# Attention with normalised queries and keys, then a gated block: one raw load placed behind two turns, and 16 more idle products

## The chip, the core and the metric

The kernel runs on one core of a Trainium2 chip. The core has a matrix engine (TensorE, PE in the profile; its weight loads are shown as PEld), a vector engine (VectorE, DVE), a scalar engine (ScalarE, ACT), a general engine (GpSimd, POOL) and SyncE (SP), which here only issues DMAs. Each engine works through its own list in order and waits on semaphores for the others. DMAs move data between the main memory, SBUF and, for the turns below, within SBUF.

The metric is the device time of one execution in microseconds (us). Before the change, three timed runs gave 277.88, 278.66 and 277.12 us, with a median of 277.88.

## The reference

Inputs are q, k and v of 8 batches, 12 heads, 448 positions and 64 numbers, and the weights of a gated block with a model width of 768 and an inner width of 1024. What is computed, cut to its core:

```
q_n = q / sqrt(mean(q*q) + 1e-6) * g_q          # over the 64 numbers; k likewise
scores = q_n @ k_n^T / 8;  attn = softmax(scores);  x = attn @ v     # heads side by side: 768 wide
h = max(x @ w_in, 0);  u, v2 = first and second 512 columns of h
v_n = (v2 - mean) / sqrt(var + 1e-6)            # over the 512 columns
gated = u * (w_spatial @ v_n + b_spatial)
out = gated @ w_out
```

The output has 8 x 448 x 768 float32 numbers.

## The kernel before

The heads are worked in 24 groups of four: group G is batch G // 3, heads 4 (G % 3) and up. A group has two raw tiles of 128 partitions x 896 float32, i = 0 for q and i = 1 for k. Each is one DMA of 448 KB.

The order of the work is written out by hand in the string `PLAN`. The loop at the end of the kernel goes through its words; each word calls the function `op_` plus its first name, and appends instructions to the lists of the engines concerned. A word such as `L.10.0/7` has the operation, its numbers (group 10, tensor 0), then the buffer or the PSUM banks, then a letter for the engine if there is a choice (a ScalarE, v VectorE, g GpSimd). So the order of the words sets the order of the instructions within every engine, and that of the DMAs in SyncE's list. Between engines there are only semaphores.

What the words mean that matter here:

- `L.G.i/slot` (line 296): a raw load of q or k of group G into one of ten raw buffers, by SyncE. `l` (line 309) is the same by halves, for group 0.
- `Q` (lines 392 and 394): the square, on ScalarE, VectorE or GpSimd. `R` (line 405) sums it, `I` and `J` (lines 418 and 423) make one over the root by a logarithm and an exponential on ScalarE. `N` (line 438) multiplies raw data by it into one of four bf16 buffers, nrm.
- `P` and `K` (lines 457, 474 to 476): for groups 0 to 3, TensorE transposes nrm and an engine copies the result out to a query or key tile.
- `T.G.i/slot` (line 493): the turn, for groups from 4 on. A transposing DMA, issued by SyncE, goes from nrm to a query tile, qT, or to a turned key tile, kr. It takes the place of `P`.
- `Z.G` (line 476): multiplies the turned keys by the two gains into the key tile kT, on VectorE or ScalarE.
- `S` (line 518): scores on TensorE, with keys on the partitions. `E` (line 526): their exponentials on ScalarE, into one of 22 tiles, et. `s`, `a` and `b` (line 553): sums and products with v on TensorE. `D`, `d`, `X` (lines 572, 576, 582): the division, into xt.
- `V`, `W`, `U`, `H`, `O` (lines 598, 627, 664, 678, 692): the gated block's products on TensorE, with `c`, `u`, `B`, `A`, `G`, `o` between them on VectorE and ScalarE. `t` stores an output tile.
- `v` (line 326), `wi` (line 333), `wo` (line 340): loads of v and of weights, issued by GpSimd.
- `z.n/f` (line 261): n idle products on an identity tile, of 128 x 64, into a spare corner of a PSUM bank. Their result is not read. The first four words of this kind stand in the first line of the plan and make one burst of 11 + 24 + 7 + 5 = 47 products.

Square, normalisation and copy of different engines are also kept in the plan's order where they use a shared port: `port` adds a semaphore between consecutive ones of VectorE and GpSimd.

SyncE's list around the change is, in order: L.10.0, L.9.1, T.4.0, T.4.1, L.8.0, T.5.1, T.5.0, L.8.1, L.11.0, L.11.1, T.6.0, T.6.1. L.10.0 is the load of the queries of group 10 into raw buffer 7. T.4.0 turns the queries of group 4, the first group that is turned by DMA, and T.4.1 its keys. The reader of L.10.0 is `Q.10.0/0/g`, a square on GpSimd.

Of the kernel before, what the change touches and what calls it, by code (L numbers as in the profile page):

```python
# [19 lines left out]
SINGLES = 4  # L20

PLAN = """
setup//v l.1.0/0 l.0.0/1 q.0.0/0/a q.1.0/1/a r.0.0//v r.1.0//v i.0//a j.0//a n.0.0//v z.11/f z.24/f z.7/f z.5/f
gl.0//g l.0.1 n.1.0//v l.1.1 q.0.1//a gl.1//g gA//v q.1.1//v r.1.1//v gB/3 L.1.1/2 r.0.1//v i.1//a Q.1.1/2/v L.1.0/3
j.1//a z.13/f Q.1.0/1/a gC//v L.2.0/4 n.0.1//v z.20/f ws//g L.2.1/5 p.1.0/2 Q.2.0/0/a p.0.0/1 Y.2/0 R.1.1//v Y.3/6
Y.0/3 k.1.0/0/v z.9/f R.1.0//v y.2//v z.8/f R.2.0//v z.4/f k.0.0/0/a y.3//v S.0.1/45 y.0//v I.1//a z.3/f J.1//a
# [8 lines left out]
b.0.1.0/0 L.12.1/8 b.0.4.0 S.2.2/12 wi.0.0//g b.1.3.0 b.1.2.0 I.4//a a.1.4.0 E.2.2/e/a s.0.2.0/4 s.0.3.0 J.4//a d.1//a  # L35
R.5.1//v s.0.4.0 S.2.4/56 a.1.3.0 wi.1.0//g E.2.4/f/a b.0.2.0 N.4.0/2/v S.2.0/12 s.0.0.0 E.2.0/g/a X.1.0//v s.0.5.0
s.0.1.0 s.0.6.0 D.0/1/a b.0.6.0 P.3.0/6 K.3.0/3/v P.3.1/5 K.3.1/3/v wi.0.2//g b.0.0.0 S.2.1/12 S.2.5/67 v.1.1//g
v.1.2//g Q.6.0/1/a b.0.5.0 Q.5.0/0/g b.0.3.0 L.10.0/7 N.4.1/3/g a.0.0.0/5 a.0.5.0 R.5.0//v s.2.2.0/4 a.0.4.0 X.1.1//v
a.0.2.0 E.2.1/h/a a.0.3.0 s.2.1.0 E.2.5/i/a S.2.3/12 I.5//a s.2.4.0 s.2.0.0 S.2.6/67 a.0.6.0 a.2.5.0/3 E.2.3/j/a
R.6.0//v J.5//a wx//v a.2.2.0 R.6.1//v s.2.5.0 S.3.0/12 a.2.3.0 a.2.4.0 Q.7.0/0/g a.0.1.0 E.2.6/k/a R.7.0//v S.3.1/67  # L40
a.2.0.0 E.3.0/l/a d.0//a a.2.6.0 s.2.6.0 b.2.1.0/2 X.0.1//v L.9.1/1 E.3.1/2/a b.2.3.0 s.2.3.0 b.2.2.0 b.2.6.0 a.2.1.0
b.2.5.0 N.5.1/1/g b.2.4.0 X.0.0//v N.5.0/0/g S.3.2/01 D.2/0/a T.4.0/1 I.6//a Q.9.1/1/g b.2.0.0 d.2//a X.2.1//v
S.3.3/67 U.0.2.1/5 E.3.3/7/a J.6//a N.6.0/2/g X.2.0//v T.4.1/0 L.8.0/6 E.3.2/5/a U.0.2.0 V.0.1.1/4 S.3.4/67 U.0.2.2
V.0.1.2 Z.4/1/v Q.7.1/2/a V.0.2.2/1 V.0.1.0 c.0.1//v E.3.4/3/a S.4.5/23 u.0.2//a S.4.0/67 E.4.5/6/a E.4.0/a/a T.5.1/1
W.0/0 c.0.3//a S.4.1/45 R.7.1//v I.7//a E.4.1/4/a S.4.2/23 N.6.1/3/g Q.10.0/0/g S.4.4/67 B.0.1//v T.5.0/0 z.1/f
L.8.1/3 z.3/f V.0.2.1 L.11.0/5 U.0.0.2/0 E.4.2/9/a B.0.3//v V.0.2.0 Z.5/0/v E.4.4/c/a U.0.0.1 U.0.0.0 S.5.1/45 J.7//a
# [718 lines left out]
```

## Time and profile before

| what | value |
|---|---|
| median of three timed runs | 277.88 us (277.12 to 278.66) |
| the profiled execution's own time | 275.78 us |
| its span, first to last instruction | 273.9 us |
| PE busy | 256.1 us (93%) |
| ACT busy | 218.0 us (80%) |
| DVE busy | 207.9 us (76%) |
| POOL busy | 136.4 us (50%) |
| mean granted TensorE clock | 0.988 |
| moved by DMA | 51.13 MB, mean 187 GB/s |

All times below are from the start of that span. The page gives busy shares of 40 equal slices of 6.85 us as a row of digits (9 is 90% or more). The chain follows the work that ended last back from the end: each piece is what released the next one, so a piece of DMA in it is a transfer that somebody had to wait for. A timeline line has start, length, engine, line, what is written from what, the shape and the number of instructions, and in brackets the idle time of the engine before it and who ended that. SPq are the issues of SyncE; the length of one is the time of issuing, not of the transfer, for which the trace has the time from issue to landing.

A busy TensorE is not one at its peak: the matrix products are pipelined. The engine's time after 66 us is nearly without gaps, and that of ScalarE in the first third is too.

### The profile page before, as it was taken

What the parts mean: (1) busy time and instruction counts of PE and PEld (TensorE: products, weight loads), DVE (VectorE), ACT (ScalarE), POOL (GpSimd) and SP (SyncE); (2) the same over time, 40 slices, a digit from 0 to 9 for tenths busy, and PEclk for the clock granted to TensorE, in tenths of its full rate; (3) what the DMA queues carried; (4) which work ended last, traced back from release to release, by engine and by line L of the source; (5) the groups of instructions that cost most, each with busy time, mean ns of one, the idle gap of its engine ahead of it and who ended that gap; (6) DMA issues with size and microseconds to landing.
All of it is one profiled execution on the core that took longest, in us unless ns stands there. A gap on an engine that the chain in (4) does not pass through costs nothing.

```text
span 273.9 us, 10070 instructions
## 1 busy us (share of the span) xinstructions
PE 256.1 (93%) x4360; PEld 134.4 (49%) x4360; DVE 207.9 (76%) x358; ACT 218.0 (80%) x359; POOL 136.4 (50%) x116
## 2 busy tenths in 40 slices
PE   3868999799999999999999999999999999999992
PEld 3734664345445554455445454454454545545551
DVE  4989995798997887989779688798547567456850
ACT  4379999799899998999899999998998974512521
POOL 3086787596978599949769614663430000000000
PEclk9989999999999999999999999999999999999997
DMA  6999999999999999999999998539197200210284
GB/s 203 329 356 254 276 261 185 297 223 221 159 259 150 331 181 191 212 284 160 296 298 208 189 247 165 85 53 190 21 130 241 80 2 2 89 57 0 85 318 176
DMA packets 62687, 51.13 MB, mean 187 GB/s; under 512 B 39217, under 2 KB 58290, under 8 KB 62642
## 3 DMA queue, kind: packets, MB, share of 16 engines
q1 hardware_dynamic: 54386, 42.22, 63.0%
q0 software_dynamic: 8256, 8.27, 20.6%
q8 instruction: 34, 0.56, 0.8%
q14 instruction: 11, 0.09, 0.2%
HBM read 38.55 MB, written 11.01 MB: 181 GB/s over the span
## 4 chain that ended last, share of the span: by engine, by line
PE 53%; ACT 14%; DMA 14%; POOL 8%; issue 6%; DVE 1%; SPq 1%; ACTq 0%; POOLq 0%; DVEq 0%
ACT et L526 10%; PE ps L553 10%; PE ps L664 9%; PE ps L692 9%; PE ps L598 8%; PE ps L678 7%; PE ps L518 7%; DMA kr<-nrm 4%; DMA w_in<-in_moe_w_in_dram 4%; PE ps L627 3%; DMA raw<-in_q_dram 3%; POOL sqt L394 3%; POOL nrm L438 3%; DMA qT<-nrm 3%; POOL vt L326 2%
## 5 line engine op out<-in xcount | busy, mean ns | idle before, releaser
L526 ACT ACTIVATE et<-ps 128x896 bf16<-128x896 f32 x168 | 145.8, 923 | 14.0 <-PE ps L518 13.2
L438 POOL TENSOR_TENSOR nrm<-raw,rs 128x896 bf16<-128x896 f32 x34 | 57.3, 1691 | 45.7 <-ACT rs L423 19.8
L518 PE MATMUL ps<-qT,kT 64*32 64x448 bf16 x1344 | 58.6, 358 | 4.3 <-DVE kT L476 2.1
L394 POOL TENSOR_TENSOR sqt<-raw 128x896 f32<-128x896 f32 x30 | 50.0, 1676 | 16.1 <-DVE vn L655 5.6
L405 DVE TENSOR_REDUCE ss<-sqt 128x14 f32<-128x896 f32 x46 | 48.7, 1073 | 2.1 <-ACT ls L418 1.1
L553 PE MATMUL ps<-et,vt 64*32 64x448 bf16 x1344 | 49.1, 349 | 0.8 <-ACT et L526 0.4
L664 PE MATMUL ps<-xt,w_in 128*128 128x448 bf16 x192 | 44.2, 353 | 0.0
L518 PEld LDWEIGHTS <-kT 64*32 64x32 bf16 x1344 | 21.3, 90 | 32.7 <-issue 23.6
L692 PE MATMUL ps<-w_out,gt 128*128 128x384 bf16 x192 | 36.8, 326 | 0.0
L598 PE MATMUL ps<-w_in,xt 128*128 128x512 bf16 x144 | 35.9, 380 | 0.0
L582 DVE TENSOR_TENSOR xt<-ps,rc 128x448 bf16<-128x448 f32 x48 | 27.9, 617 | 8.1 <-PE ps L553 4.0
L553 PEld LDWEIGHTS <-vt 64*32 64x32 bf16 x1344 | 24.2, 92 | 14.5 <-issue 3.4
L373 ACT ACTIVATE os<-ps 128x384 f32<-128x384 f32 (+1 forms) x37 | 17.6, 492 | 14.5 <-PE ps L692 8.5
L553 PE MATMUL ps<-et,ones 64*32 64x448 bf16 x672 | 28.1, 349 | 0.0
L678 PE MATMUL ps<-w_spT,vn 128*128 128x448 bf16 (+1 forms) x128 | 27.6, 353 | 0.1
L664 PEld LDWEIGHTS <-w_in 128*128 128x128 bf16 x192 | 17.2, 98 | 19.0 <-issue 5.3
L692 PEld LDWEIGHTS <-gt 128*128 128x128 bf16 x192 | 17.9, 98 | 15.9 <-issue 3.4
L639 DVE BATCH_NORM_STATS2 s<-vs 128x6 f32<-128x512 bf16 (+1 forms) x32 | 21.8, 682 | 3.3 <-ACT vs L589 2.8
L683 DVE TENSOR_TENSOR gt<-ps,us 128x448 bf16<-128x448 f32 x32 | 19.2, 618 | 6.6 <-PE ps L678 6.0
L326 POOL DMA_DIRECT2D vt<-in_v_dram x34 | 23.2, 683 | 1.8 <-DMA w_in<-in_moe_w_in_dram 1.5
L375 DVE COPY os<-ps 128x384 f32<-128x384 f32 (+1 forms) x26 | 14.2, 554 | 9.7 <-PE ps L692 4.0
L598 PEld LDWEIGHTS <-xt 128*128 128x128 bf16 x144 | 13.0, 98 | 16.7 <-issue 3.8
(62 smaller groups left out, 257.2 us busy)
## 6 DMA issues: line engine op xcount, KB each, us to landing
raw<-in_k_dram SPq DMA_DIRECT2D x23, 448.0 KB, 6.8
raw<-in_q_dram SPq DMA_DIRECT2D x23, 448.0 KB, 7.0
out_dram<-os SPq DMA_DIRECT2D x24, 384.0 KB, 3.7
vt<-in_v_dram POOLq DMA_DIRECT2D x14, 224.0 KB, 6.1
vt<-in_v_dram POOLq DMA_DIRECT2D x20, 112.0 KB, 5.3
w_in<-in_moe_w_in_dram POOLq DMA_DIRECT2D x8, 192.0 KB, 9.7
out_dram<-os SPq DMA_DIRECT2D x7, 192.0 KB, 4.6
w_out<-in_moe_w_out_dram POOLq DMA_DIRECT2D x1, 768.0 KB, 8.1
```

Of the source, the lines that this page charges most:

```text
L326: pool.dma_start(out=vts[b % 2][64 * halves[0]:64 * halves[0] + 64 * len(halves), g].rearrange("p r c d -> p r (c d)"), in_=src)
L394: port(eng, eng.tensor_tensor(out=t, in0=x, in1=x, op=ALU.mult))
L405: dve.tensor_reduce(out=sss[G % 3][:, i].rearrange("p r c -> p (r c)"), in_=sqt[where.pop(("sq", G, i))].rearrange("p r (c d) -> p (r c) d ...
L438: port(eng, eng.tensor_tensor(out=nrm[sl[0]].rearrange("p c r d -> p r c d"), in0=raw[where["raw", G, i]].rearrange("p r (c d) -> p r c d" ...
L518: pe.matmul(out=ps[at:at + 32, sl[n], 0:S], lhsT=kT[64 * r:64 * r + 64, c, 64 * hh + 32 * x:64 * hh + 32 * x + 32], rhs=qT[64 * r:64 * r + ...
L526: act.activation(out=ets[sl[0]].rearrange("q r (p c) -> q r p c", c=C), in_=ps[:, a:b + 1:b - a, 0:S].rearrange("q r (c p) -> q r p c", c= ...
L553: pe.matmul(out=ps[32 * l:32 * l + 32, where[kind, G][0], 0:S], lhsT=w, rhs=et_of(G, r, c)[at:at + 64], start=(n == 1), stop=(n == C), til ...
L582: dve.tensor_tensor(out=xts[b % 2][:, 2 * g + half, :], in0=ps[:, where.pop(("ab"[half], G))[0], 0:S], in1=rcs[where["rc", G]], op=ALU.mult)
L598: pe.matmul(out=ps[:, bank, :], lhsT=xts[b % 2][:, j, 128 * m:128 * m + 128], rhs=w_in[:, j % 2, j // 2, DH:], start=(n == 1 and j == 2 * ...
L664: pe.matmul(out=ps[:, bank, 0:S], lhsT=w_in[:, j % 2, j // 2, 128 * f:128 * f + 128], rhs=xts[b % 2][:, j, :], start=(n == 1 and j == 2 * ...
L678: pe.matmul(out=ps[:, sl[0], 0:S], lhsT=vns[b % SLOTS["vn"]][rows, m, 128 * f:128 * f + 128], rhs=w_spT[rows, m, :], start=(m == 0), stop= ...
L692: pe.matmul(out=ps[:, sl[0], 0:384], lhsT=gts[b % 2][:, f, 128 * m:128 * m + 128], rhs=w_out[:, f, 384 * h:384 * h + 384], start=(f == 0), ...
```

## The change

Two words of the plan change. The load of group 10's queries, `L.10.0/7`, is taken from its place between `b.0.3.0` and `N.4.1/3/g` and put behind `T.4.1/0`, in front of `L.8.0/6`. In SyncE's list it so goes behind L.9.1, T.4.0 and T.4.1. And `z.24/f` in the first line becomes `z.40/f`, so that the first burst has 63 idle products. The lists of VectorE, ScalarE and GpSimd are the same; that of TensorE has 16 more weight loads and products at its start. The other lines of the diff only break the text anew and are left out.

```diff
-setup//v l.1.0/0 l.0.0/1 q.0.0/0/a q.1.0/1/a r.0.0//v r.1.0//v i.0//a j.0//a n.0.0//v z.11/f z.24/f z.7/f z.5/f
+setup//v l.1.0/0 l.0.0/1 q.0.0/0/a q.1.0/1/a r.0.0//v r.1.0//v i.0//a j.0//a n.0.0//v z.11/f z.40/f z.7/f z.5/f
...
-v.1.2//g Q.6.0/1/a b.0.5.0 Q.5.0/0/g b.0.3.0 L.10.0/7 N.4.1/3/g a.0.0.0/5 a.0.5.0 R.5.0//v s.2.2.0/4 a.0.4.0 X.1.1//v
+v.1.2//g Q.6.0/1/a b.0.5.0 Q.5.0/0/g b.0.3.0 N.4.1/3/g a.0.0.0/5 a.0.5.0 R.5.0//v s.2.2.0/4 a.0.4.0 X.1.1//v a.0.2.0
...
-S.3.3/67 U.0.2.1/5 E.3.3/7/a J.6//a N.6.0/2/g X.2.0//v T.4.1/0 L.8.0/6 E.3.2/5/a U.0.2.0 V.0.1.1/4 S.3.4/67 U.0.2.2
+U.0.2.1/5 E.3.3/7/a J.6//a N.6.0/2/g X.2.0//v T.4.1/0 L.10.0/7 L.8.0/6 E.3.2/5/a U.0.2.0 V.0.1.1/4 S.3.4/67 U.0.2.2
```

In the new SyncE list the order is: L.9.1, T.4.0, T.4.1, L.10.0, L.8.0, T.5.1, T.5.0, and from there on as before.

## The prediction

> **What bounds the kernel now.** I read the slices of the page first, then the chain, then the timeline of the stretch the edit touches. The page puts TensorE at 256.1 us of a 273.9 us span, yet the early slices are not full, so the question is what holds TensorE back where the diff works.
>
> ```profile
> PE   3868999799999999999999999999999999999992
> ACT  4379999799899998999899999998998974512521
> ```
>
> Slice 7 (48 to 55 us) drops to 7 tenths on TensorE and ScalarE alike, between full slices. The chain names the cause: one turn of a key tile, "kr", from its issue to its landing, then the vector copy of that tile, then scores, then exponentials.
>
> ```profile
> 40.17 8.79 DMA kr<-nrm
> 49.06 0.46 DVE kT L476
> 49.57 0.43 PE ps L518 x8
> 50.02 1.73 ACT et L526 x2
> 55.37 7.23 ACT et L526 x9
> ```
>
> Columns are start, length, what. The turn is T.4.1 of the plan. The timeline (start, length, engine, line, then in brackets the idle time before it) shows all three engines waiting at once, and SyncE's queue ahead of that:
>
> ```profile
> 33.39 0.37 SPq L296 DMA_DIRECT2D raw<-in_q_dram  x1
> 35.39 0.37 SPq L296 DMA_DIRECT2D raw<-in_k_dram  x1
> 35.85 4.23 SPq L493 DMA_TRANSPOSE qT<-nrm  x1
> 40.17 3.33 SPq L493 DMA_TRANSPOSE kr<-nrm  x1
> 43.55 1.08 SPq L296 DMA_DIRECT2D raw<-in_q_dram  x1
> 44.73 1.24 SPq L493 DMA_TRANSPOSE kr<-nrm  x1
> 46.05 3.15 SPq L493 DMA_TRANSPOSE qT<-nrm  x1
> ...
> 49.06 0.45 DVE L476 TENSOR_SCALAR kT<-kr,g_col 128x896 bf16<-128x896 bf16 x1 [3.83 <-DMA kr<-nrm]
> 49.57 0.57 PE L518 MATMUL ps<-qT,kT 64*32 64x448 bf16 x16 [2.08 <-DVE kT L476]
> 50.02 1.73 ACT L526 ACTIVATE et<-ps 128x896 bf16<-128x896 f32 x2 [1.94 <-PE ps L518]
> ```
>
> In order these are L.10.0 (moved by the edit), L.9.1, T.4.0, T.4.1, L.8.0, T.5.1, T.5.0. Issuing T.4.0 took 4.23 us where a turn issued into a shorter queue took 1.23 (the one at 57.08), so the transfers ahead of it were still in the way. The cost is 2.08 us on TensorE and 1.94 on ScalarE. Is it won back later? The windows view says no (busy us of PE, PEld, DVE, ACT, POOL with counts):
>
> ```profile
> 48.00:54.00 6.00, 4.43 (x59) 2.05 (x60) 4.55 (x9) 4.06 (x8) 3.99 (x3) 1.00 1.10 287
> 54.00:60.00 6.00, 6.00 (x92) 2.24 (x94) 6.00 (x8) 6.00 (x10) 4.93 (x3) 1.00 1.14 230
> 60.00:66.00 6.00, 5.88 (x172) 3.45 (x165) 4.85 (x10) 6.00 (x13) 5.39 (x6) 1.00 1.16 237
> ```
>
> From 50.02 to 66 us ScalarE has no idle time, and at 66.11 the chain passes to TensorE, which is full. Time saved before 50 us moves all that follows.
>
> **The change part by part.**
>
> *The load L.10.0.* One DMA of 448 KB goes from ahead of L.9.1, T.4.0 and T.4.1 to behind them. Nothing is added to SyncE's list, and POOL, DVE and ACT keep their order.
>
> (a) L.9.1 waits for its buffer, which the vector engine frees at 35.36 (nrm, 34.28 + 1.08), so its issue stays at 35.39. It lands sooner: now 9.8 us after issue, at 45.18, and POOL's square of it starts at 45.34 after 1.48 us idle. POOL's 1.48 is not on the chain, so I count nothing for it.
>
> (b) T.4.0 stays at 35.85, but with 448 KB less in front. T.4.1 reads the POOL normalisation of 37.09 to 38.77 and was held from 38.77 to 40.17 by the issue of T.4.0; up to 1.4 us of that can go.
>
> (c) How much sooner does T.4.1 land? It lands when the bytes ahead have passed. Lower bound: early loads with nearly nothing beside them land 1.2 us apart (raw q issued at 3.11 and 3.62 land at 11.30 and 12.50). Upper bound: of the loads issued at 31.39, 33.39 and 35.39 the first lands at 40.41 and the last at 45.18, so two took 4.77, or 2.4 each, but POOL's loads of v (landing at 44.08 and 45.08) shared that. They still have to be moved, so 2.4 is too much. I take the rate at which all queues moved in the window 36 to 42 us, 271 GB/s: 458,752 B / 271 GB/s = 1.69 us, between the ends. T.4.1 then lands at 48.96 - 1.69 = 47.27, its copy ends near 47.8 and scores start near 47.9 instead of 49.57. TensorE is free from 47.49 and ScalarE from 48.08, so the gain cannot pass 1.94 us; 1.69 fits under it. Ends: 1.2 and 1.94.
>
> (d) L.10.0 itself is issued near 41.8 (T.4.1's issue ended at 43.50; less 1.7). Its reader is POOL's square at 51.24, near 49.5 if everything moves up. L.8.0, at the head of the same place now, lands 6.5 us after its issue; 41.8 + 6.5 = 48.3, in time. At the longest latency of a load in this ramp, 11.8 us, it would be 53.6; POOL idles 2.15 us before its work at 55.07, so the square could start at 53.39 without loss. Cost 0, covered by that idle time; without it, one for one.
>
> (e) L.8.0, T.5.1 and T.5.0 now have L.10.0 just ahead of them, but the same bytes in all. They land at 50.02, 50.80 and 51.59. Their readers start at 53.42 (square on DVE), 53.07 (copy on DVE) and 54.39 (scores); 1.69 sooner, 51.7, 51.4 and 52.7. Still after the landings, by 0.6 us at the least. Cost 0, and that 0.6 is the cover.
>
> *The 16 idle products.* The first burst has 47 in 2.69 us, 57 ns each, ending at 4.38; the next TensorE work waits for a vector result until 7.76.
>
> ```profile
> 1.69 2.69 PE L261 MATMUL ps<-ident 128*128 128x64 bf16 x47 [1.69 <-POOL ident masks.py:199]
> 7.76 0.58 PE L384 MATMUL ps<-one_f,g_row 1*128 1x1 f32 x2 [3.39 <-DVE g_row L379]
> 8.28 1.94 PE L261 MATMUL ps<-ident 128*128 128x64 bf16 x33
> 12.55 0.79 PE L261 MATMUL ps<-ident 128*128 128x64 bf16 x21
> ```
>
> 16 x 57 ns = 0.91 us, so the burst ends at 5.29, inside the 3.39 us of idle time. Cost 0; if that gap were gone, 0.91. A gain is bounded too: products take 59 ns at 8.28 and 38 ns at 12.55, so a quick clock at 8.28 would save 33 x 21 ns = 0.7 us. But ScalarE's copy of the first query tile at 13.38 stands behind a square that waits for a raw load to land at 12.50, so I take 0.
>
> *The sum.* -1.69 + 0 = -1.7 us. The profiled execution took 275.78 us (span 273.9 and 1.9 around it), so it would take 274.1. The median of the three timed runs is 277.88, 2.1 above it, with a spread of 1.5 us that this profile does not explain. On the median: 276.2 us. About 0.5%, 1.4 us, is what a measurement of this kernel can tell from no change.
>
> **The rivals.**
>
> *Half the gain.* POOL's loads of v were issued at 32.09 and 34.02, land 12.0 and 11.1 us later, and run beside the turns. If every second piece that moves into the freed room is POOL's, T.4.1 gains 1.69 / 2 = 0.85 us: 277.0. The two landings speak for it; against it, those bytes have passed by 45.08 in any case. The Trainium skill, "DMA: Bandwidth & Descriptors", section "Queues, rings and completion order", states that each DMA engine takes turns between the queues it has work for, one packet at a time. By that rule the sum would be -0.85; the trace agrees that both queues' transfers are under way together, and no row here shows the alternation itself.
>
> *Taken back or hidden.* T.4.1 lands sooner, but a later wait eats it, say one of the stretches from 112 to 155 us where the chain runs through POOL and ScalarE, or the transfers' pace does not change at all: 277.9. Between 43 and 48 us they move only 55 to 260 GB/s (55 from 47 to 48), so this stretch is not limited by bytes alone; that is for it. Against it: the full engines after 54 us.
>
> *Slower: the second pair of turns comes late.* With two loads in a row ahead, T.5.1 and T.5.0 become what T.4.0 and T.4.1 are now. It takes gain away once T.5.1 lands after 51.4, and turns to a loss once T.5.1 lands after 53.07 or T.5.0 after 54.39. At T.4.0's 10.15 us from issue to landing, T.5.0, issued at 46.05, lands at 56.2, and the scores that began at 54.39 begin 1.8 later: 279.7. For it: T.4.0 and T.4.1 have just this history (two loads ahead, 10.15 and 8.79). Against it: POOL's loads, which ran beside those, have landed by 45.08.
>
> *The warm-up counts.* The clock quickens before 8.28 and the chain feels it: 0.7 more, 275.5. Against it stands the 12.50 landing. The Trainium skill, "TensorE: Matmul & The Clock Gate", Part 1, says the full clock comes after about 3.4 us of sustained work, seen in free-running windows. 2.69 us fall short and 3.6 us can reach it, so by that rule the 33 products run quick; the trace agrees so far that the first 47 stay slow.
>
> **How the numbers follow.** Full forecast 0.45 (own range 275.7 to 276.8, as its gain lies between 1.2 and 1.94 us and measurement adds some; about 0.06 of it falls within 0.5%), half the gain 0.14, taken back 0.14, slower 0.22, warm-up 0.05. So faster 0.39 + 0.05 = 0.44, same 0.06 + 0.14 + 0.14 = 0.34, slower 0.22. The range starts at 275.3, just under the warm-up case, and reaches to 279.0, into the slower one, leaving out about 0.15 of it above and 0.04 below.
>
> **What would show it.** Right: T.4.1 issued before 39.5 and landing near 47.3; TensorE's wait for kT under 0.6 us; POOL's square that waits at 45.34 starting near 44; slice 7 at 9; the first burst of 63 products with 7.76 unchanged. Wrong: T.4.1 still landing after 48.5; a new wait of TensorE on kT at 52 to 56 us (the second pair), or of POOL for L.10.0 after 51; or the gain there at 55 us and gone at 160.

## The result and the profile after

| | before | changed |
|---|---|---|
| median of 10 timed runs | 277.60 us (275.63 to 278.66) | 275.36 us (274.15 to 276.76) |
| ratio, 95% interval | | 0.992 (0.989 to 0.995) |
| profiled execution: own time, span | 275.78, 273.9 us | 275.58, 273.8 us |

The change is faster by 2.2 us on the median; 276.2 us was forecast. The two profiled executions are nearly equal in time, though, and this has to be understood before they are compared. First the slices of TensorE and ScalarE after the change:

```profile
PE   5859999999999999999999999999999999999991
ACT  4277999999899999899889999998988974511621
```

Slice 7 is at 9 on both, where it was at 7. But two early slices, counted from 0, have lost: TensorE's slice 2 is at 5 where it was at 6, and ScalarE's slice 3 at 7 where it was at 9. The windows view (columns as before: busy us of PE, PEld, DVE, ACT and POOL, granted clock, DMA share, GB/s) confirms the filled slice 7. ScalarE has no gap from 48 to 60 us, and from 48 to 54 us TensorE lacks 0.12 us where it lacked 1.57:

```profile
48.00:54.00 6.00, 5.88 (x66) 2.64 (x65) 4.65 (x9) 6.00 (x10) 4.34 (x3) 1.00 1.13 248
54.00:60.00 6.00, 6.00 (x95) 2.25 (x94) 6.00 (x8) 6.00 (x10) 4.95 (x4) 1.00 1.11 271
```

The timeline of the same stretch after the change: SyncE's queue, GpSimd's square of L.9.1 and its normalisation for group 6, then the copy of the key tile, scores and exponentials.

```profile
36.94 0.37 SPq L296 DMA_DIRECT2D raw<-in_k_dram  x1
37.36 2.12 SPq L493 DMA_TRANSPOSE qT<-nrm  x1
40.35 2.41 SPq L493 DMA_TRANSPOSE kr<-nrm  x1
42.81 2.61 SPq L296 DMA_DIRECT2D raw<-in_q_dram  x2
45.52 1.22 SPq L493 DMA_TRANSPOSE kr<-nrm  x1
...
45.69 1.68 POOL L394 TENSOR_TENSOR sqt<-raw 128x896 f32<-128x896 f32 x1 [0.28 <-DMA raw<-in_k_dram]
47.32 1.69 POOL L438 TENSOR_TENSOR nrm<-raw,rs 128x896 bf16<-128x896 f32 x1
49.05 0.45 DVE L476 TENSOR_SCALAR kT<-kr,g_col 128x896 bf16<-128x896 bf16 x1 [1.81 <-POOL nrm L438]
49.55 0.57 PE L518 MATMUL ps<-qT,kT 64*32 64x448 bf16 x16
50.01 1.73 ACT L526 ACTIVATE et<-ps 128x896 bf16<-128x896 f32 x2
```

The waits of 2.08 us (TensorE) and 1.94 us (ScalarE) are gone. Yet the exponentials begin at 50.01, where they began at 50.02. The work ahead of them was late: L.9.1 was issued at 36.94 instead of 35.39, and the exponential that started at 45.09 before starts at 47.07 now. What the change saves at 48 us, this execution had lost earlier.

ScalarE's list is the same, in the same order, in every kernel here, so the start of its n-th activation (counted from 0; the loading of its table at the start is not counted) can be laid side by side. The first row has times from the trace of before, the others the difference to it; the kernels under the second one are the experiments below.

| n | 8 | 24 | 40 | 56 | 72 | 136 | 168 | 357 |
|---|---|---|---|---|---|---|---|---|
| before, us | 12.52 | 26.29 | 35.86 | 45.09 | 57.64 | 97.23 | 119.72 | 268.89 |
| changed | +0.86 | +1.56 | +1.55 | +1.98 | -0.02 | -0.03 | -0.56 | -0.58 |
| load alone (e1) | +0.08 | +1.49 | +1.48 | +1.66 | -0.41 | -0.42 | -0.95 | -0.96 |
| products alone (e2) | +0.91 | +1.62 | +1.61 | +1.97 | +2.38 | +2.37 | +1.84 | +3.23 |
| products later (f2) | +0.86 | +0.86 | +2.00 | +1.89 | +0.51 | +0.50 | +0.04 | +0.24 |
| load between (e3) | +0.48 | +1.18 | +1.18 | +1.18 | +2.63 | +2.53 | +2.01 | +2.00 |
| load later (f3) | +0.21 | +0.73 | +0.73 | +0.73 | +2.42 | +2.62 | +2.09 | +2.45 |
| gaps filled (e4) | -0.07 | +1.10 | +1.09 | +1.09 | -0.13 | +1.17 | +0.69 | +5.18 |
| gaps filled, same count (f4) | -0.42 | -0.41 | -0.41 | -0.41 | -1.65 | -1.66 | -1.75 | -1.76 |

Two things are read from it. Between n = 56 and 72 the kernels with the load behind both turns and in front of the second pair gain 1.2 to 2.1 us on the trace of before; f1, g1, g2 and g3 below, which are not in the table, gain 1.94, 1.65, 2.06 and 1.32. The kernels e2, e3 and f3 lose there. But f2, which has the load where it was before, gains 1.38. So one execution of each kernel does not tell what the load is worth, and f2 is taken up below. And the profiled execution of before had an early ramp, the stretch up to n = 56: it is ahead of all others but one there. That fits its own time, which stood 1.8 us under the median of its kernel; that the ramp is the reason is not shown, since there is one trace of that kernel.

### The profile page after: what moved, and what is told of

Its sections match the earlier page's. It is cut to its first block, busy times and chain, and to the rows that moved or that the text cites. A ratio compares the mean times of both kernels' runs of the same rounds, so it can differ in the third digit from the quotient of the medians.

```text
span 273.8 us, 10088 instructions
## 1 busy us (share of the span) xinstructions
PE 257.5 (94%) x4363; PEld 135.5 (50%) x4376; DVE 207.9 (76%) x358; ACT 218.0 (80%) x359; POOL 136.3 (50%) x116
## 4 chain that ended last, share of the span: by engine, by line
PE 58%; ACT 12%; issue 8%; DVE 8%; POOL 6%; DMA 6%; SPq 1%; ACTq 0%; POOLq 0%; DVEq 0%
PE ps L553 12%; ACT et L526 10%; PE ps L664 9%; PE ps L692 8%; PE ps L518 8%; PE ps L598 8%; PE ps L678 8%; POOL sqt L394 3%; DMA raw<-in_k_dram 3%; PE ps L627 3%; DMA kr<-nrm 3%; POOL nrm L438 2%; DVE ss L405 2%; POOL vt L326 1%; PE ps L457 1%
## 5 line engine op out<-in xcount | busy, mean ns | idle before, releaser
L438 POOL TENSOR_TENSOR nrm<-raw,rs 128x896 bf16<-128x896 f32 x34 | 57.3, 1689 | 46.9 <-ACT rs L423 18.8
L518 PE MATMUL ps<-qT,kT 64*32 64x448 bf16 x1344 | 60.1, 362 | 3.0 <-ACT qT L373 1.7
L405 DVE TENSOR_REDUCE ss<-sqt 128x14 f32<-128x896 f32 x46 | 48.7, 1073 | 3.0 <-POOL sqt L394 1.8
L553 PE MATMUL ps<-et,vt 64*32 64x448 bf16 x1344 | 48.7, 350 | 0.4 <-ACT et L526 0.4
L598 PE MATMUL ps<-w_in,xt 128*128 128x512 bf16 x131 | 34.3, 380 | 0.6
```

What stands on the lines that cost most here:

```text
L405: dve.tensor_reduce(out=sss[G % 3][:, i].rearrange("p r c -> p (r c)"), in_=sqt[where.pop(("sq", G, i))].rearrange("p r (c d) -> p (r c) d ...
L438: port(eng, eng.tensor_tensor(out=nrm[sl[0]].rearrange("p c r d -> p r c d"), in0=raw[where["raw", G, i]].rearrange("p r (c d) -> p r c d" ...
L518: pe.matmul(out=ps[at:at + 32, sl[n], 0:S], lhsT=kT[64 * r:64 * r + 64, c, 64 * hh + 32 * x:64 * hh + 32 * x + 32], rhs=qT[64 * r:64 * r + ...
L553: pe.matmul(out=ps[32 * l:32 * l + 32, where[kind, G][0], 0:S], lhsT=w, rhs=et_of(G, r, c)[at:at + 64], start=(n == 1), stop=(n == C), til ...
L598: pe.matmul(out=ps[:, bank, :], lhsT=xts[b % 2][:, j, 128 * m:128 * m + 128], rhs=w_in[:, j % 2, j // 2, DH:], start=(n == 1 and j == 2 * ...
```

## The experiments

Each ran beside the kernel before. The medians of before were 277.05 us for the kernels named e, 277.40 for f and 277.03 for g. The ratios are taken over the runs of each kernel and are not the quotients of the medians.

**The load alone, e1.** The changed kernel with the first burst of idle products as before:

```diff
-z.40/f
+z.24/f
```

> Only the load L.10.0 is moved, the burst keeps 47 products. Theory 'load' (T.4.1 lands sooner because 448 KB no longer stand ahead of it; that is the whole gain of 2.2 us): 275.4 to 275.8 us on the median, TensorE's wait for kT before the scores of group 4 (2.08 us before) under 0.6 us. Rival 'products' (the longer burst moves the clock, and that is the gain): 277.3 to 277.9 us, and the wait for kT gone or not makes no difference at the end. Rival 'both': 276.2 to 276.7.

Measured: 276.14 us, ratio 0.998 (0.995 to 1.001), so not clear of no change in this comparison. The wait for kT is nil in its profile (no line of that name among TensorE's waits from 42 to 60 us), and the table shows 2.07 us gained at that place. The timing fell between the theory and "both".

**The products alone, e2.** On the kernel before:

```diff
-z.24/f
+z.40/f
```

> Only the 16 products are added, the load stays where it was. Theory 'load': 277.4 to 277.9 us, the wait for kT still about 2 us or, where the ramp ran at the slow clock for longer, smaller by what the ramp lost. Rival 'products': 275.4 to 275.8. Rival 'both': 276.3 to 276.8. In the profile the clock should show full speed from about 5 us, as in the profile of the changed kernel (5.1 us), if the burst is long enough for that.

Measured: 276.32 us, ratio 0.996 (0.992 to 1.000). The wait stays. TensorE's waits in its profile (us in total, times, longest):

```profile
PE ps L518 <- DVE kT L476: 2.5, 1, 2.5
PE ps L518 <- issue: 0.2, 1, 0.2
```

In this execution the products do not touch what the load repairs. It is the slowest of its kernel, though: 279.0 us, where the median is 276.32. The products' own share was left open here: the timing allows up to 2 us, the profile shows none at this place.

**The load between the two turns, e3.** On the kernel before:

```diff
-b.0.3.0 L.10.0/7 N.4.1/3/g
+b.0.3.0 N.4.1/3/g
...
-T.4.0/1 I.6//a
+T.4.0/1 L.10.0/7 I.6//a
```

> The load goes behind T.4.0 but ahead of T.4.1, burst of 47. Theory 'load' in the form that what counts is the bytes ahead of T.4.1: no gain, 277.3 to 277.9 us, and T.4.1 lands where it did. In the form that two turns side by side with loads ahead are what is slow (they cannot run while some transfers lag): half the gain or more, 276.0 to 276.8. If the load between two turns adds another change-over between loads and turns (transfers moved only 55 to 170 GB/s from 46 to 48 us): slower than before, 278.2 to 279.

Measured: 277.47 us, ratio 1.001 (0.999 to 1.004), and the wait is there as before. The issue of T.4.1 now takes the time that T.4.0's took:

```profile
36.99 1.73 SPq L493 DMA_TRANSPOSE qT<-nrm  x1
38.77 0.62 SPq L296 DMA_DIRECT2D raw<-in_q_dram  x1
39.98 4.19 SPq L493 DMA_TRANSPOSE kr<-nrm  x1
...
50.70 0.57 PE L518 MATMUL ps<-qT,kT 64*32 64x448 bf16 x16 [2.04 <-DVE kT L476]
```

What counts is that the load stands ahead of T.4.1, which is the form of the theory that the prediction used; whether by its 448 KB or as one more transfer in the queue, no run separates. That two turns next to each other are slow for themselves is not borne out: half the gain or more was expected from it when the load parts them, and none came. The table shows e3 losing 1.45 us between n = 56 and 72 although the wait is no longer than before. Part of that can be the clock: this trace grants TensorE half of it from 51.28 to 54.70 us, that of before all of it.

**Idle products in the ramp's gaps, e4.** On the load alone:

```diff
-z.4/f k.0.0/0/a
+z.16/f k.0.0/0/a
...
-S.0.0/01 N.1.0/0/g
+S.0.0/01 z.16/f N.1.0/0/g
...
-P.1.0/2 E.0.0/0/a
+P.1.0/2 z.16/f E.0.0/0/a
```

> Load moved, burst of 47, and 12, 16 and 16 idle products more in TensorE's gaps between 13 and 18.2 us, so that the stretch of half clock that follows (18.23 to 21.64 us before, 15.38 to 25.62 in the profile of the changed kernel) does not come. If the half clock in the ramp costs time at the end: 0.5 to 1.5 us under the load alone, 274.2 to 275.2, and the clock row of the page has 9 in the third and fourth slice. If ScalarE and the transfers pace the ramp whatever the clock: the same as the load alone within 0.4 us.

Measured: 281.86 us, ratio 1.018 (1.013 to 1.022): neither expectation. The stretch from 42 to 66 us is fine (n = 72 at -0.13), and the loss comes later, in four stops of TensorE's weight loads. One timeline line behind each of them:

```profile
76.08 0.14 PEld L518 LDWEIGHTS <-kT 64*32 64x32 bf16 x15 [1.53 <-issue]
132.99 1.23 PEld L678 LDWEIGHTS <-vn 128*128 128x128 bf16 x7 [1.14 <-issue]
168.44 1.06 PEld L678 LDWEIGHTS <-vn 128*128 128x128 bf16 x7 [2.08 <-issue]
213.59 0.10 PEld L518 LDWEIGHTS <-kT 64*32 64x32 bf16 x6 [1.29 <-issue]
```

"issue" means that nothing shown by the profile held them. Counted from 0, the stopped weight loads are numbers 1245, 2269, 2908 and 3676. The distances are 1024, 639 and 768: eight, five and six times 128, but for one in the middle.

**The same idle products at an unchanged count, f4.** On e4:

```diff
-z.24/f
+z.8/f
...
-z.13/f
+z.1/f
...
-z.20/f
+z.4/f
```

> As e4_fill, with 44 products taken out of the first three bursts, so that from 19 us on every instruction stands at the same place of TensorE's list as with the load alone. Theory 'place in the list' (e4_fill was slow by stops of 1.2 to 2.2 us at four places that lie 128 weight loads times a whole number apart, because TensorE's instructions come in blocks of 16 KB and came late): 275.6 to 276.6 us, and the stops gone. Rival 'the idle products themselves' (the ramp's other state, or the clock): 279.5 to 282.

Measured: 275.64 us, ratio 0.994 (0.990 to 0.997). TensorE's waits from 66 to 270 us are down to these two:

```profile
PE ps L518 <- DMA qT<-nrm: 0.2, 1, 0.2
PE ps L518 <- ACT et L526: 0.2, 1, 0.2
```

The 44 products in the gaps cost nothing if 44 are taken out ahead of them. So the loss of e4 came from the place of the later instructions in TensorE's list. That they wait for their own code is an inference at first: the page counts 34 packets and 0.56 MB on the "instruction" queue, and 0.56 MB / 8,720 TensorE instructions are 64 B each, so a packet holds 256 of them, or 128 weight loads with their products. The Trainium skill ("Runtime: NRT & Kernel Launch", "Instruction fetch mechanics") states that an engine's instructions are fetched in blocks of 16 KiB, or 256, and that crossing from one to the next is mostly hidden. The size agrees with 0.56 MB / 34 packets; that it is hidden does not hold for the four places in e4, if they are fetches.

The DMA records of e4's trace support that they are. One packet of 16,384 B of that queue lies just ahead of each stop: they end at 74.68, 131.62, 167.16 and 212.24 us, that is 1.3 to 1.4 us before the weight load that was held starts. The restored count is no full protection either. The repeat g3 of this same kernel has one stop of 1.53 us, at 106.50 us, 1.54 us after such a packet's end, and it is weight load 1757, four times 128 behind the first of e4. What makes a packet late was not tested.

**Both parts again, f1.** The changed kernel as it is, beside the f kernels.

> Both parts again, beside the same runs of the kernel before as the next three. Load alone gave 276.14 and products alone 276.32 where the kernel before gave 277.05. If the two parts add up: 275.2 to 275.6 us. If only the load counts and the products' 0.7 us was scatter: 275.9 to 276.4.

Measured: 275.76 us, ratio 0.995 (0.993 to 0.998). The time lies between the two expectations, 275.2 to 275.6 and 275.9 to 276.4.

**The products in a later burst, f2.** On before:

```diff
-z.20/f
+z.36/f
```

> The load stays where it was and the 16 products go into the burst of 20 that follows the one of 13, so 36 there and 47 in the first burst. TensorE's list is as long as with the products alone and every later instruction stands at the same place in it, but the early burst is not longer. Theory 'early clock' (the first burst's length is what helps): 276.9 to 277.4 us, as before. Theory 'place in the list' (what helps is that the later instructions are shifted against the blocks in which TensorE's instructions are fetched): 276.1 to 276.5, as with the products alone. Theory 'scatter': anywhere within 0.7 us of before.

Measured: 277.04 us, ratio 0.998 (0.995 to 1.001). It fits the early clock and the scatter alike, and e2's interval and this one overlap, so it decides nothing by itself. Its profile shows something else. The load is where it was before, and yet the wait is short:

```profile
PE ps L518 <- DVE kT L476: 0.7, 1, 0.7
```

Counted from ScalarE's activation 56, T.4.1 landed 1.6 us sooner here than in before. So the wait that the change removes differs from execution to execution, from 0.7 to 2.5 us in the three with the load in its old place.

**Load alone and both side by side, g1 and g2.** The kernels of e1 and f1 once more.

> The load alone once more, in one session with both parts, since so far they were timed in different ones (ratios to before 0.998 and 0.995). Theory 'load, and the products do nothing': the two medians within 0.3 us of each other. Theory 'both add': 0.4 to 0.8 us above the next.

> Both parts, beside the load alone. Theory 'load, and the products do nothing': the same median within 0.3 us. Theory 'both add': 0.4 to 0.8 us under the load alone. In either case 1.3 to 2.3 us under the kernel before.

Measured: 275.60 us, ratio 0.995 (0.992 to 0.998), for the load alone, and 275.91 us, ratio 0.997 (0.994 to 1.000), for both. Within 0.31 us, and the order is the other way round. The products add nothing that these runs can tell; the 0.7 us of e2 did not show on top of the load, and the products alone were not timed again. Both parts are 1.1 us under before here, a little less than the 1.3 to 2.3 expected.

**The load behind the second pair too, f3.** On the load alone:

```diff
-T.4.1/0 L.10.0/7 L.8.0/6
+T.4.1/0 L.8.0/6
...
-T.5.1/1
+T.5.1/1 T.5.0/0 L.10.0/7
...
-B.0.1//v T.5.0/0 z.1/f
+B.0.1//v z.1/f
```

> Burst of 47; the load goes further back, behind T.5.1 and T.5.0 as well (T.5.0 is requested right behind T.5.1, its order in the queue unchanged), so that the second pair of turns has one load ahead instead of two. If the second pair limits the gain of the load alone: 0.5 to 1.5 us under it, 274.6 to 275.6. If it has slack, as the prediction has it: the same as the load alone, 275.8 to 276.5. If the reader of L.10.0 on POOL becomes late (issue near 48, landing near 53): slower than the load alone by up to 1, 276.6 to 277.2.

Measured: 278.33 us, ratio 1.003 (1.000 to 1.007), above even the slowest expectation. The second pair did not need the room. The load became late, and its lateness went where nobody had looked:

```profile
52.31 1.68 POOL L394 TENSOR_TENSOR sqt<-raw 128x896 f32<-128x896 f32 x1 [2.18 <-DMA raw<-in_q_dram]
...
54.03 0.45 DVE L476 TENSOR_SCALAR kT<-kr,g_col 128x896 bf16<-128x896 bf16 x1 [2.03 <-POOL sqt L394]
54.53 0.76 PE L518 MATMUL ps<-qT,kT 64*32 64x448 bf16 x24 [1.22 <-DVE kT L476]
```

VectorE's copy Z.5, whose keys had long landed, waited for GpSimd's square of L.10.0, because the kernel keeps the plan's order between the two engines on their shared port. Not all of the loss in this trace is that wait: from 56.67 to 60.08 us it grants TensorE half the clock.

**The reader of the load behind that copy, g4.** On f3, with every engine's own list unchanged:

```diff
-N.6.1/3/g Q.10.0/0/g S.4.4/67
+N.6.1/3/g S.4.4/67
...
-Q.8.0/2/v L.11.1/2
+Q.8.0/2/v Q.10.0/0/g L.11.1/2
```

> As f3_load_later (278.33 us), but the square that reads L.10.0 stands in the plan behind VectorE's copy Z.5 and the square Q.8.0, so that Z.5 no longer has to wait for it by the order that is kept between GpSimd and VectorE. Every engine's own list is the same. If the loss there came from Z.5 waiting for a square that waited for a late load: Z.5's wait of 2.03 us goes, 275.8 to 277 us. If it came from the late load holding up GpSimd itself, or from the turns: 278 to 279.

Measured: 277.27 us, ratio 0.999 (0.996 to 1.002). The copy no longer waits:

```profile
54.03 0.44 DVE L476 TENSOR_SCALAR kT<-kr,g_col 128x896 bf16<-128x896 bf16 x1
54.39 1.08 DVE L394 TENSOR_TENSOR sqt<-raw 128x896 f32<-128x896 f32 x1
```

On the medians 1.1 us of f3's 278.33 come back, about half of the distance to the load alone. The two intervals, 1.000 to 1.007 and 0.996 to 1.002, overlap, so the size is uncertain. The time is a little over the range expected. The square now starts at 55.60, after 3.36 us in which GpSimd was idle; that this is the rest of the price is a guess.

**The filled gaps once more, g3.** The kernel of f4.

> The kernel with the load moved, 44 products taken from the first three bursts and put into the gaps from 13 to 18 us, again. If what it showed once (275.64, and a span of 272.6 us) is more than scatter, 0.2 to 0.8 us under both parts; if not, the same as both within 0.3.

Measured: 275.59 us, ratio 0.997 (0.994 to 1.000): 0.32 us under both parts in the median, and the same in the ratio. No version here beats the changed kernel by an amount that the runs can tell.

## Why the prediction was right, step by step

**The forecast.** It gave a gain of 1.7 us, and 2.2 were measured in the first comparison. The time measured there, 275.36 us, lies under the range that the prediction gave to its full forecast, 275.7 to 276.8, just above the 275.3 at which its whole range starts, and nearest to the case of the warm-up, 275.5, whose effect the runs do not show. Part of that is the start: the ten runs of before have a median 0.28 us under that of the three. The rest is luck of the first comparison. Both parts gave ratios of 0.992, 0.995 and 0.997, the load alone 0.998 and 0.995. Their mean, 0.9956, is a gain of some 1.2 us: at the lower end that the prediction named, 1.2 to 1.94 us. For the profiled execution 274.1 us was forecast, and it took 275.58, with a ramp that was later by 1.98 us.

The cause named, the load ahead of the turns, stands. With the load alone the gain is clear of no change in g1, though not in e1; with the load in front of T.4.1 there is none (e3); and the products add nothing to it (g1, g2). The path from the load to the gain was only in part the one named. Seven kernels or repeats with the load moved and four others show it, in us from ScalarE's activation 56 of the same execution:

| | T.4.1 lands | GpSimd's normalisation ends | the copy Z.4 starts | TensorE waits for kT |
|---|---|---|---|---|
| before | 3.9 | 3.6 | 4.0 | 2.1 |
| products alone (e2) | 4.0 | 4.3 | 4.4 | 2.5 |
| products later (f2) | 2.2 | 2.6 | 2.6 | 0.7 |
| load between (e3) | 3.8 | 2.3 | 3.9 | 2.0 |
| changed, f1, g2 | 1.6, 1.6, 0.0 | 1.9, 2.0, 1.9 | 2.0, 2.0, 1.9 | 0.1 or less |
| load alone: e1, g1 | 0.1, 1.9 | 1.9, 2.3 | 1.9, 2.3 | 0, 0.4 |
| same count: f4, g3 | 2.6, 2.3 | 2.1, 2.6 | 2.7, 2.6 | 0.8, 0.8 |

The copy starts at whichever of the two comes last. With the load moved it starts 1.9 to 2.7 us after activation 56, 2.2 on average; with the load in its old place at 4.0, 4.4 and 2.6, on average 3.6. The difference, 1.4 us, is near to what the timing gives. But the two groups touch, by f2, and three executions are few.

**Step (c), T.4.1 sooner by 1.69 us.** Right in sign, and its size differs with the execution. In the changed kernel T.4.1 is issued at 40.35 and lands 8.3 us later, near 48.7; ScalarE's work there runs 1.98 us later than before, so against that work it lands some 2.3 us sooner (48.96 - 48.7 + 1.98). With the load alone it is issued at 40.28 and takes 6.6 us: 46.9, or 3.7 us sooner by the same reckoning. In f4 it is 1.2 us sooner, and in f2, with the load not moved, 1.6. In the changed kernel and in e1 the cap of 1.94 us, from ScalarE's idle time, was about what came: 2.00 and 2.07 us were gained at that place. The signs named for it in absolute times (issue before 39.5, landing near 47.3, the square near 44) did not come, and one sign of being wrong, a landing after 48.5, did: 48.66. This execution's ramp was late by 1.55 us at n = 40 and 1.98 at n = 56, which accounts for it.

**Step (a), GpSimd's 1.48 us "not on the chain".** This was wrong, and hidden by luck. In the profile before, GpSimd's normalisation ended at 46.98 + 1.69 = 48.67, only 0.29 us ahead of the landing at 48.96, and the copy Z.4 also waits for it by the port's order. Had T.4.1 alone come sooner, 0.29 us would have been the gain. It was more because L.9.1 came sooner too: GpSimd's square waits 0.28 us for it now. In the changed kernel the copy is released by that normalisation and no longer by the landing ("1.81 <-POOL nrm" above), and it is the same with the load alone. Nor is it so only after the change. With the load in its old place the normalisation came last in e2, where the square before it waited 2.07 us for L.9.1 and the normalisation itself 0.51 us more:

```profile
51.45 0.45 DVE L476 TENSOR_SCALAR kT<-kr,g_col 128x896 bf16<-128x896 bf16 x1 [4.23 <-POOL nrm L438]
```

**Step (b)** holds: the issue of T.4.0 takes 2.12 us where it took 4.23, and T.4.1 is issued at 40.35, right after its input is done (38.64 + 1.68 = 40.32).

**Step (d), the load's own lateness free.** Right for this place: the square starts at 51.23 without a wait. Its cover was wrong. It counted 2.15 us of GpSimd's idle time. But the copy Z.5 waits for that square too, and in the trace of before it started at 53.07, 0.15 us after the square's end (51.24 + 1.68). f3 shows the square handing its lateness on to that copy, and in g4, where this link is undone, about half of the loss comes back.

**Step (e) and the slower rival.** No wait of TensorE for the second pair's keys shows from 50 us on. In f3, where the pair had one load less ahead, nothing was gained by it. The rival had the right sign for a load that is put too far back, and the wrong place.

**The products.** Cost 0, as said: 63 take 3.54 us and end at 5.22; the next work starts at 7.64. The rival "the warm-up counts" has its condition met in some executions, and its effect does not show. In e2 the 33 products behind the gap took 1.14 us where they took 1.94 before, and ScalarE's activation 8 still came 0.91 us later, not sooner. Windows of the changed kernel, cut where the clock changes (the first one is shown at full clock because no change is recorded before its end, but its 63 products take 56 ns each):

```profile
0.00:5.10 5.10, 3.42 (x63) 3.39 (x63) 1.84 (x10) 2.33 (x3) 2.46 (x9) 1.00 0.61 163
5.10:8.50 3.40, 0.98 (x24) 0.85 (x22) 2.75 (x6) 1.10 (x3) 0.00 (x0) 1.00 1.07 262
8.50:12.00 3.50, 3.44 (x56) 3.09 (x52) 1.79 (x3) 0.52 (x2) 0.00 (x0) 0.51 0.98 335
12.00:15.40 3.40, 1.43 (x41) 1.26 (x42) 3.40 (x7) 2.79 (x4) 0.00 (x0) 1.00 1.06 384
15.40:25.60 10.20, 8.35 (x112) 4.57 (x105) 9.17 (x13) 7.20 (x12) 8.17 (x10) 0.50 1.08 282
```

The full clock comes at 5.1 us, as the rule in the Trainium skill ("TensorE: Matmul & The Clock Gate", Part 1, some 3.4 us of sustained work, seen in free-running windows) has it. The trace agrees: TensorE has worked 3.42 us by then, and the next changes follow 3.4 us apart. The full clock lasts for one window of 3.4 us, in which TensorE is busy 0.98 us, and is gone before its first transposes, at 9.35 us. In g2 the same 63 products did not bring it at all: the 33 products at 8.25 us take 59 ns each there, and the first change to full clock on record is at 23.4 us.

**The rivals "half the gain" and "taken back".** The first is not refuted. Its 0.85 us would be a ratio of 0.997, which is the mean of the two comparisons of the load alone; all five give 1.2 us, between it and the 1.69 forecast. That the pieces of two queues alternate, its mechanism, no run here shows. The gain is not taken back: f1 and g1 are clear of no change at the end of the kernel, and from n = 72 to 357 the changed kernel and e1 each gain another 0.56 us on the trace of before. e3, with nothing gained at the load's place, does much the same there (0.64), so that belongs to the execution of before.

## What to carry to other kernels

Before an early landing is booked as a gain, list every wait of the instruction that needs it, with the time at which each was met: here a second one stood 0.29 us behind the first, and the gain was only had because the same edit moved both. A load's slack is not the idle time of the engine that reads it; follow the semaphores that its reader releases on other engines as well. And compare executions by the n-th instruction of an engine whose list did not change: one table shows where each gains and loses, while the spans, 273.8 and 273.9 us, showed nothing. Do it for several executions of each kernel: f2 alone would have said that the load does not matter, and e1 alone that it is worth 2 us.

## What the runs showed of the hardware that was not expected

- The place in TensorE's list matters. 44 products more ahead of the main part cost 1.8%, with four stops of 1.1 to 2.1 us that begin multiples of 128 weight loads apart, but for one load, each just behind a packet of the instruction queue; with the count restored there was none over 1 us in f4 and one of 1.53 us in g3.
- The ramp differs from execution to execution. ScalarE's activation 56 came from 0.41 us earlier to 2.30 us later than in the trace of before, over all profiles of these kernels. It does not simply follow the clock: with the load alone the first change to full clock on record comes at 23.3 us, in the changed kernel at 5.1, and they are 1.66 and 1.98 us late.
